# Eight heads instead of four per group in a decode attention kernel: 8 MiB V tiles, K in two halves, a mask for the own head

## The chip, the cores and the metric

The kernel runs on one core of a Trainium2 chip. The core has a matrix engine (TensorE, PE in the profile, with its weight loads as PEld), a vector engine (VectorE, DVE), a scalar engine (ScalarE, ACT), a general engine (GpSimd, POOL), and a queue engine (SyncE, SP) that here only issues transfers. Sixteen DMA engines move data from the device memory (HBM) into the on-chip memory of 128 partitions (SBUF). PE writes to the accumulator memory PSUM. The metric is the device time of one execution in microseconds, lower is better.

## The reference, cut to what matters

One decode step for 8 sequences: attention over a cache of 4096 keys and 32 heads of width 128, gated against a small MLP on the same x.

```
B, Sq, D = 8, 1, 576
H, Sk, Dh = 32, 4096, 128
q = (x @ wq).reshape(B, Sq, H, Dh).transpose(0, 2, 1, 3)
scores = einsum("bhqd,bhkd->bhqk", q, k_cache) * (Dh ** -0.5)
o = einsum("bhqk,bhkd->bhqd", softmax(scores), v_cache)
a = o.transpose(0, 2, 1, 3).reshape(B, Sq, H * Dh) @ wo
b = gelu(layernorm(x) @ w1 + b1) @ w2 + b2
out = g * a + (1 - g) * b          # g = sigmoid(sum(x * gate_w))
```

K and V caches are bf16, 268.4 MB each. All weights together are some 20 MB. With one query per sequence every byte of K and V is used once.

## The kernel before, in words

A group g is one batch row and HB = 4 heads; NG = 64 groups, batch row innermost. K and V of a group are 4 MiB each. They lie in SBUF with a head on 32 partitions, 128 consecutive keys on each partition (NTT = 128), so that one partition row is 32 KB and contiguous in HBM, and the whole tile is one contiguous stretch of 4 MiB. There are two buffers for K (KB) and two for V (VB).

The instructions of each engine stand in an order written out by hand; `op` records them, with the producers that each waits for. For a group:

- `q_of`: PE spreads q of the group's four heads over the partitions with a selection matrix, ACT copies it to q_bc.
- `scores`: the keys are worked in four chunks of 32 keys per partition. Per chunk, `mult` lets DVE multiply K by q (L354, 128x4096 elements) into one of the two halves of p1, PE sums that in eight matmuls against the identity (L364), and `reduce` lets DVE add the last 16 values (L369) into s_sb. The fourth multiply of a group frees its K buffer (`k_done`).
- `softmax`: DVE takes the maximum of each head (L387 to L393), then ACT runs four exp, one per head and its 32 partitions (L396), into P. P holds for each key a row of four head columns, of which only the own head's is ever written; the others stay zero from a memset at the start.
- `rowsum`, `total`: DVE sums P over the keys (L402), PE adds over partitions (L421).
- `pv`: PE multiplies P with V in 32 matmuls of 16 columns by 512 (L414); the last one frees the V buffer (`v_done`). `evict` copies the result out (L427), `gather` picks the own head's rows in four matmuls (L432), `norm` divides (L438, L439).

These steps are staggered: `rowsum`, `total`, `pv` and `evict` of group g-1 run inside the scores of group g, `norm` of g-2 too.

The transfers of K and V (`load_k` L223, `load_v` L229) stand in SP's one queue. At group g, K of g+1 is issued (it waits until K of g-1 is used up), then V of g (it waits for `pv` of g-2). SP issues strictly in order.

The MLP and the two projections ride along: `up_proj` in groups 3 to 14, `act_h` and the load of w2 at group 15, `down_proj` in groups 19 to 24, `b_out` and the load of wo at group 25, `a_proj` for each set of four heads once all batch rows are normalised. The weights share the buffer RB one after another.

At the end, V of the last group comes in seven pieces of falling size (V_LAST: 32, 32, 16, 16, 16, 8, 8 keys per partition). It is used by `pv_turned` (L508), which makes V the stationary operand and P the four moving columns, one matmul per key row, 128 in all, so that its result needs no gather. After the last piece come `norm_turned` (L517), the last `a_proj` (L477), the final mix (L593) and four small stores.

Of the kernel before, what the change touches and what calls it, by code (L numbers as in the profile page):

```python
# [11 lines left out]
B = 8  # L12
# [9 lines left out]
HB = 4  # L22
NHG = H // HB
NG = NHG * B
NTT = SK // 32
CT = 32
NCK = NTT // CT
# [5 lines left out]
NTQ = NTT // TQ  # L33

# [50 lines left out]
def bass_gated_mix__mha_block_cached__mixer_channel_mlp__decode_kernel(  # L85
# [41 lines left out]
    p1 = sb("p1", [128, 2, CT, DH], BF16)  # L127

# [20 lines left out]
    up = sb("up", [128, 2, NJ * B], F32)  # L149
    Q4 = sb("Q4", [128, NHG * DH], BF16)  # L150
    Sel = sb("Sel", [128, B, 128], BF16)
    q_bc = sb("q_bc", [128, 2, DH], BF16)
    OT_sb = sb("OT_sb", [128, H, B], BF16)
    bmg_sb = view(up, 0, [128, QN])
# [4 lines left out]
    sel16 = sb("sel16", [128, TQ, HB], F32)  # L159
    stat = sb("stat", [B, 16], F32)  # L160
    s_sb = sb("s_sb", [128, 2, NTT], F32)
# [3 lines left out]
    mD = sb("mD", [128, 2, 32], F32)  # L165
    gm = sb("gm", [128, 1], F32)
    P = sb("P", [128, 2, NTT, HB], BF16)
    rs = sb("rs", [128, 2, HB], F32)
# [14 lines left out]
    sV = [nc.alloc_semaphore(f"sV{i}") for i in range(2)]  # L183
    nK, nV = [0, 0], [0, 0]
# [8 lines left out]
    def bcast(t):  # L193
# [6 lines left out]
    ld_b2 = [load("scalar", b2_4[32 * i:32 * i + B, :],  # L200
                  bass.AP(tensor=B_b2.tensor, offset=B_b2.offset + i * QN, ap=[[0, B], [1, QN]]), f"ld_b2{i}", [c_b2])
             for i in range(4)]
# [9 lines left out]
    def kv_src(cache, g):  # L212
        hg, b = divmod(g, B)
        return cache[b, hg * HB:(hg + 1) * HB].rearrange("h (p t) d -> (h p) t d", p=32)

# [3 lines left out]
    def load_k(g):  # L219
        s = g % 2  # L220
        nK[s] += 1
        src = kv_src(A_k_cache, g)
        k_land[g] = op("sync", lambda e: e.dma_start(KB[s][:, :, :], src), [k_done.get(g - 2)], dma=(sK[s], 16 * nK[s]))  # L223

    def load_v(g):
        s = g % 2
        nV[s] += 1
        src = kv_src(A_v_cache, g)
        t = op("sync", lambda e: e.dma_start(VB[s][:, :, :], src), [v_done.get(g - 2)], dma=(sV[s], 16 * nV[s]))  # L229
        v_land[g] = [(t, 0, NTT)]  # L230
# [3 lines left out]
    def load_v_pieces(g):  # L234
        s = g % 2
        src = kv_src(A_v_cache, g)
        v_land[g] = []
        t0 = 0
        for n, nt in enumerate(V_LAST):
            dst, part = VB[s][:, t0:t0 + nt, :], src[:, t0:t0 + nt, :]  # L240
            t = load("sync", dst, part, f"sVl{n}", [v_done.get(g - 2)])
            v_land[g].append((t, t0, t0 + nt))
            t0 += nt
        assert t0 == NTT

    load_k(0)
    load_v(0)
    load_k(1)


    def memset(engine, ap, value):
# [9 lines left out]
    c_P = memset("gpsimd", P[:], 0.0)  # L261
    c_ps = [memset("vector", bank[i][:, :], 0.0) for i in range(4)]
    c_yps = memset("vector", y_ps[:, :], 0.0)
    c_sel16 = op("vector", lambda e: e.tensor_reduce(
        out=sel16[:].rearrange("p t h -> p (t h)"),
        in_=bass.AP(tensor=ident, offset=0, ap=[[pstride(ident), 128], [1, TQ * HB], [32, 4]]),
        axis=AX.X, op=ALU.add), [c_id])
    c_Sel = op("vector", lambda e: e.tensor_copy(
        out=Sel[:].rearrange("p b (h r) -> p b h r", h=HB),
        in_=bass.AP(tensor=ident, offset=0, ap=[[pstride(ident), 128], [1, B], [32, HB], [0, 32]])), [c_id])  # L270
# [54 lines left out]
    for half in range(2):  # L325
        for h in range(HB):
            for kt in range(NKT):
                o = tr_ps[half][32 * h:32 * h + B, :]
                at = (kt * SK + half * (SK // 2) if kt < NKF else NKF * SK) + h * DH
                r = bass.AP(tensor=RB, offset=at, ap=[[pstride(RB), 128], [HB * DH, 4], [1, DH]])  # L330
# [11 lines left out]
    a_qb, v_mult, v_red, p_sum, v_nm, a_exp, p_pv, a_ev, p_oz, v_norm, v_rs, p_z, v_rz = ({} for _ in range(13))  # L342

    def q_of(g):
        hg, b = divmod(g, B)
        t = op("tensor", lambda e: e.matmul(qb_ps[:, 0:DH], lhsT=Sel[:, b, :], rhs=Q4[:, hg * DH:(hg + 1) * DH],  # L346
                                            start=True, stop=True), [a_Q[hg // 4], c_Sel, a_qb.get(g - 1)])
        a_qb[g] = op("scalar", lambda e: e.activation(out=q_bc[:, g % 2, :], in_=qb_ps[:, 0:DH], func=ACT.Copy),  # L348
                     [t, v_mult.get((g - 2, NCK - 1))])

    def mult(g, c):
        s, par = g % 2, c % 2
        qb = bass.AP(tensor=q_bc, offset=q_bc[:, s, :].offset, ap=[[pstride(q_bc), 128], [0, CT], [1, DH]])
        v_mult[g, c] = op("vector", lambda e: e.tensor_tensor(  # L354
            out=p1[:, par, :, :], in0=KB[s][:, c * CT:(c + 1) * CT, :], in1=qb, op=ALU.mult),
            [k_land[g], a_qb[g], p_sum.get((g, c - 2) if c >= 2 else (g - 1, c + NCK - 2))]
            + ([v_yT, p_yT, p_Q] if g == 0 and c < 2 else []))
        if c == NCK - 1:
            k_done[g] = v_mult[g, c]
        for n in range(NCH):  # L360
            r = bass.AP(tensor=p1, offset=p1[:, par, 0, n * CH:n * CH + 1].offset,
                        ap=[[pstride(p1), 128], [DH, CT], [1, CH]])
            w = [v_mult[g, c], v_red.get((g, c - 2) if c >= 2 else (g - 1, c + NCK - 2)), *a_Q] if n == 0 else ()
            p_sum[g, c] = op("tensor", lambda e, r=r, n=n: e.matmul(  # L364
                tr_ps[par][:, :], lhsT=ident[:, :], rhs=r, start=(n == 0), stop=(n == NCH - 1)), w)

    def reduce(g, c):
        s, par = g % 2, c % 2
        v_red[g, c] = op("vector", lambda e: e.tensor_reduce(  # L369
            out=s_sb[:, s, c * CT:(c + 1) * CT], in_=tr_ps[par][:, :].rearrange("p (t c) -> p t c", c=CH),  # L370
            axis=AX.X, op=ALU.add), [p_sum[g, c], a_exp.get(g - 2)])

    def scores(g, between):

        mult(g, 0)
        between(0)
        mult(g, 1)
        between(1)
        for c in range(NCK):
            reduce(g, c)  # L380
            if c + 2 < NCK:
                mult(g, c + 2)
                between(c + 2)

    def softmax(g):
        s = g % 2
        t = op("vector", lambda e: e.tensor_reduce(out=mA[:, 0:1], in_=s_sb[:, s, :], axis=AX.X, op=ALU.max),  # L387
               [v_red[g, NCK - 1], c_mA])
        t = op("vector", lambda e: e.transpose(mB[:, :], mA[:, :]), [t])  # L389
        t = op("vector", lambda e: e.tensor_reduce(out=gm[:, :], in_=mB[:, :], axis=AX.X, op=ALU.max), [t])  # L390
        gmb = bass.AP(tensor=gm, offset=0, ap=[[pstride(gm), 128], [0, 32]])
        t = op("vector", lambda e: e.tensor_scalar(out=mC[:, :], in0=gmb, scalar1=-1.0, scalar2=None, op0=ALU.mult), [t])
        v_nm[g] = op("vector", lambda e: e.transpose(mD[:, s, :], mC[:, :]), [t, a_exp.get(g - 2)])  # L393
        for h in range(HB):
            q = slice(32 * h, 32 * h + 32)
            a_exp[g] = op("scalar", lambda e, h=h, q=q: e.activation(  # L396
                out=P[q, s, :, h], in_=s_sb[q, s, :], func=ACT.Exp, bias=mD[q, s, 0:1], scale=1.0),
                [v_nm[g], p_pv.get(g - 2), v_rs.get(g - 2), c_P])

    def rowsum(g):  # L400
        s = g % 2
        v_rs[g] = op("vector", lambda e: e.tensor_reduce(  # L402
            out=rs[:, s, :], in_=P[:, s, :, :].rearrange("p t h -> p h t"), axis=AX.X, op=ALU.add),
            [a_exp[g], p_z.get(g - 2)])

    def pv(g, part, parts):
        s = g % 2
        for land, t0, t1 in v_land[g]:
            t0, t1 = max(t0, part * NTT // parts), min(t1, (part + 1) * NTT // parts)
            for tq in range(t0 // TQ, t1 // TQ):  # L410
                j = tq % 4
                o = o_ps[s][32 * j:32 * j + TQ * HB, :]
                w = [land, a_exp[g], a_ev.get(g - 2), *c_ps] if tq == t0 // TQ else ()
                p_pv[g] = op("tensor", lambda e, o=o, tq=tq: e.matmul(  # L414
                    o, lhsT=P[:, s, tq * TQ:(tq + 1) * TQ, :].rearrange("p t h -> p (t h)"),
                    rhs=VB[s][:, tq * TQ:(tq + 1) * TQ, :].rearrange("p t d -> p (t d)"),
# [216 lines left out]
```

## Time and profile before

| | |
|---|---|
| runs of the kernel, median (lowest to highest) | 1310.96 us (1310.36 to 1311.30) |
| span of the profiled execution, first to last instruction | 1308.8 us |
| HBM bytes read | 556.96 MB |
| mean rate over the span | 426 GB/s |
| DVE / PE / ACT busy | 66% / 64% / 16% |
| mean granted PE clock | 0.818 |

The profiled execution's own time is its span; the median of the runs is 2.16 us above that span. The page of the profile gives the busy time of each engine, the span in 40 slices, the DMA queues, the chain of work that ended last, the costliest groups of instructions and the DMA issues. In a row of a group, the first figure after the bar is the busy time in us, the second the mean of one instruction in ns, and what follows the second bar is the engine's idle time just before them and what ended it.

### The profile page before, as it was taken

What the parts mean: (1) busy time and instruction counts of PE and PEld (TensorE: products, weight loads), DVE (VectorE), ACT (ScalarE), POOL (GpSimd) and SP (SyncE); (2) the same over time, 40 slices, a digit from 0 to 9 for tenths busy, and PEclk for the clock granted to TensorE, in tenths of its full rate; (3) what the DMA queues carried; (4) which work ended last, traced back from release to release, by engine and by line L of the source; (5) the groups of instructions that cost most, each with busy time, mean ns of one, the idle gap of its engine ahead of it and who ended that gap; (6) DMA issues with size and microseconds to landing.
All of it is one profiled execution on the core that took longest, in us unless ns stands there. A gap on an engine that the chain in (4) does not pass through costs nothing.

```text
span 1308.8 us, 12641 instructions
## 1 busy us (share of the span) xinstructions
PE 843.5 (64%) x5428; PEld 384.4 (29%) x5428; DVE 869.7 (66%) x1061; ACT 204.1 (16%) x393; POOL 2.5 (0%) x13
## 2 busy tenths in 40 slices
PE   3567766766746666646766766765766665766766
PEld 1223433433312233212322222322322222322323
DVE  4576676676747667646766766766776666776675
ACT  1201111111210110101011111011111111111111
POOL 0000000000000000000000000000000000000000
PEclk8878888878868888768878878878878878878878
DMA  9999999999999999999999999999999999999997
GB/s 398 422 431 432 431 432 431 432 431 430 434 424 432 430 431 429 428 418 432 429 431 429 431 431 431 431 432 430 432 430 431 431 431 429 432 431 432 429 420 311
DMA packets 25255, 557.77 MB, mean 426 GB/s; under 512 B 2528, under 2 KB 6640, under 8 KB 7536
## 3 DMA queue, kind: packets, MB, share of 16 engines
q1 hardware_dynamic: 24944, 556.95, 99.4%
q8 instruction: 42, 0.69, 0.2%
q14 instruction: 13, 0.11, 0.0%
q10 hardware_dynamic: 256, 0.03, 0.0%
HBM read 556.96 MB, written 0.01 MB: 426 GB/s over the span
## 4 chain that ended last, share of the span: by engine, by line
DMA 69%; DVE 20%; PE 10%; SPq 0%; issue 0%; ACT 0%
DMA KB<-in_A_k_cache_dram 68%; DVE p L354 16%; PE psb L364 10%; DVE s_sb L369 3%; DMA VB<-in_A_v_cache_dram 1%; SPq L187 0%; PE psb L414 0%; ACT L467 0%; SPq L229 0%; DVE mA L387 0%; SPq L223 0%; PE psb L477 0%; DVE mB L389 0%; ACT O_sb L427 0%; DVE gm L390 0%
## 5 line engine op out<-in xcount | busy, mean ns | idle before, releaser
L364 PE MATMUL psb<-p,ident 128*128 128x512 bf16 x2048 | 610.9, 459 | 412.2 <-DVE p L354 411.8
L354 DVE TENSOR_TENSOR p<-KB,q_bc 128x4096 bf16<-128x4096 bf16 x256 | 579.6, 2285 | 278.0 <-DMA KB<-in_A_k_cache_dram 278.0
L364 PEld LDWEIGHTS psb<-p,ident 128*128 128x128 bf16 x2048 | 218.1, 114 | 744.5 <-DVE p L354 445.2
L369 DVE TENSOR_REDUCE s_sb<-psb 128x32 f32<-128x512 f32 x256 | 176.1, 688 | 129.9 <-PE psb L364 129.6
L427 ACT ACTIVATE O_sb<-psb 128x512 f32<-128x512 f32 x63 | 37.6, 597 | 1032.2 <-PE psb L414 1032.2
L396 ACT ACTIVATE P<-s_sb,mD 32x128 bf16<-32x128 f32 x256 | 147.0, 574 | 12.9 <-DVE mD L393 9.0
L414 PE MATMUL psb<-VB,P 128*16 128x512 bf16 x2016 | 119.9, 379 | 0.3 <-DMA VB<-in_A_v_cache_dram 0.3
L432 PE MATMUL psb<-sel,O_sb 128*128 128x4 f32 x504 | 66.9, 256 | 32.9 <-ACT O_sb L427 32.9
L432 PEld LDWEIGHTS psb<-sel,O_sb 128*128 128x128 f32 x504 | 61.6, 192 | 41.3 <-ACT O_sb L427 41.2
L414 PEld LDWEIGHTS psb<-VB,P 128*16 128x16 bf16 x2016 | 44.7, 89 | 70.4 <-issue 26.3
L402 DVE TENSOR_REDUCE rs<-P 128x4 f32<-128x512 bf16 x64 | 43.5, 680 | 2.1 <-ACT P L396 2.1
L421 PEld LDWEIGHTS psb<-rs,ones 128*128 128x128 f32 x128 | 24.4, 192 | 9.3 <-issue 0.4
L348 ACT ACTIVATE q_bc<-psb 128x128 bf16<-128x128 f32 x64 | 17.4, 272 | 32.7 <-PE psb L346 32.7
L452 PEld LDWEIGHTS psb<-yT_sb,RB 128*128 128x128 bf16 (+1 forms) x216 | 19.4, 165 | 3.4
L452 PE MATMUL psb<-yT_sb,RB 128*128 128x8 bf16 (+1 forms) x216 | 19.8, 227 | 0.0
L387 DVE TENSOR_REDUCE mA<-s_sb 128x1 f32<-128x128 f32 x64 | 18.3, 286 | 2.2
L421 PE MATMUL psb<-rs,ones 128*128 128x4 f32 x128 | 18.4, 214 | 0.0
L389 DVE STREAM_TRANSPOSE mB<-mA 128x32 f32<-128x32 f32 x64 | 13.6, 213 | 2.2
L393 DVE STREAM_TRANSPOSE mD<-mC 128x32 f32<-128x32 f32 x64 | 13.6, 212 | 2.2
L346 PE MATMUL psb<-Q,Sel 128*128 128x128 bf16 x64 | 14.7, 229 | 0.0
L346 PEld LDWEIGHTS psb<-Q,Sel 128*128 128x128 bf16 x64 | 6.1, 96 | 27.0 <-issue 26.8
L390 DVE TENSOR_REDUCE gm<-mB 128x1 f32<-128x32 f32 x64 | 11.9, 186 | 2.2
(63 smaller groups left out, 84.7 us busy)
## 6 DMA issues: line engine op xcount, KB each, us to landing
KB<-in_A_k_cache_dram SPq DMA_DIRECT2D x64, 4096.0 KB, 27.2
VB<-in_A_v_cache_dram SPq DMA_DIRECT2D x63, 4096.0 KB, 33.1
RB<-in_B_w_dram SPq DMA_DIRECT2D x1, 5184.0 KB, 44.3
RB<-in_B_w_dram SPq DMA_DIRECT2D x1, 4608.0 KB, 36.6
RB<-in_A_wo_dram SPq DMA_DIRECT2D x1, 4608.0 KB, 44.7
RB<-in_A_wq_dram SPq DMA_DIRECT2D x1, 4096.0 KB, 12.8
VB<-in_A_v_cache_dram SPq DMA_DIRECT2D x2, 1024.0 KB, 8.7
VB<-in_A_v_cache_dram SPq DMA_DIRECT2D x3, 512.0 KB, 11.2
```

What stands on the lines that cost most here:

```text
L346: t = op("tensor", lambda e: e.matmul(qb_ps[:, 0:DH], lhsT=Sel[:, b, :], rhs=Q4[:, hg * DH:(hg + 1) * DH], start=True, stop=True), [a_Q[hg ...
L354: v_mult[g, c] = op("vector", lambda e: e.tensor_tensor(out=p1[:, par, :, :], in0=KB[s][:, c * CT:(c + 1) * CT, :], in1=qb, op=ALU.mult), ...
L364: p_sum[g, c] = op("tensor", lambda e, r=r, n=n: e.matmul(tr_ps[par][:, :], lhsT=ident[:, :], rhs=r, start=(n == 0), stop=(n == NCH - 1)), w)
L369: v_red[g, c] = op("vector", lambda e: e.tensor_reduce(out=s_sb[:, s, c * CT:(c + 1) * CT], in_=tr_ps[par][:, :].rearrange("p (t c) -> p t ...
L387: t = op("vector", lambda e: e.tensor_reduce(out=mA[:, 0:1], in_=s_sb[:, s, :], axis=AX.X, op=ALU.max), [v_red[g, NCK - 1], c_mA])
L396: a_exp[g] = op("scalar", lambda e, h=h, q=q: e.activation(out=P[q, s, :, h], in_=s_sb[q, s, :], func=ACT.Exp, bias=mD[q, s, 0:1], scale=1.0),
L402: v_rs[g] = op("vector", lambda e: e.tensor_reduce(out=rs[:, s, :], in_=P[:, s, :, :].rearrange("p t h -> p h t"), axis=AX.X, op=ALU.add), ...
L414: p_pv[g] = op("tensor", lambda e, o=o, tq=tq: e.matmul(o, lhsT=P[:, s, tq * TQ:(tq + 1) * TQ, :].rearrange("p t h -> p (t h)"), rhs=VB[s] ...
L421: p_z[g] = op("tensor", lambda e: e.matmul(oz_ps[:, HB:2 * HB], lhsT=ones[:, :], rhs=rs[:, g % 2, :], start=True, stop=True), [v_rs[g], v_ ...
L427: a_ev[g] = op("scalar", lambda e: e.activation(out=O_sb[:].rearrange("p t d -> p (t d)"), in_=o_ps[s][:, :], func=ACT.Copy), [p_pv[g], p_ ...
L432: p_oz[g] = op("tensor", lambda e, tt=tt: e.matmul(oz_ps[:, 0:HB], lhsT=O_sb[:, tt, :], rhs=sel16[:, tt, :], start=(tt == 0), stop=(tt == ...
L452: st["p_up"] = op("tensor", lambda e, w=w, o=o, kt=kt: e.matmul(o, lhsT=w, rhs=yT_sb[:, kt, :], start=(kt == 0), stop=(kt >= NKF)), [*ld_w ...
```

## The change

HB becomes 8, so there are 32 groups n. A head now has 16 partitions, with 256 consecutive keys on each (NTT = 256).

- V of a group is one transfer of 8 MiB with 64 KB per partition, into one buffer of that size; there is no second V buffer. V of n+1 waits until `pv` of n is done.
- K of a group comes in two halves of the keys (units u = 2n and 2n+1), each 4 MiB with 32 KB rows that lie 64 KB apart in HBM. The two K buffers stay as they were; the first half's buffer is free after the fourth multiply, the second's after the eighth.
- `scores` runs eight chunks. `softmax` has one exp over all 128 partitions and 256 keys into E; then DVE multiplies E eight times by a column of `own` (1 where the partition belongs to the head, else 0), which writes all eight head columns of P. The row sum is one reduce of E and a multiply with `own`.
- `pv` has 64 matmuls with 32 columns; `total`, `pv`, `evict` and `gather` of a group now follow its softmax at once, before the next group's scores; `norm` comes in the next group's second chunk.
- q is broadcast once per batch row for all 32 heads (8 times instead of 64).
- SP's order at the end of group n: both halves of K of n+1, then V of n+1. At the start K0, K1, V0. In the last two groups: first half of V of 30, both K halves of 31, second half of V of 30, first half of V of 31 into the first K buffer, then the seven pieces with the second half of V of 31 into VB.
- At the end: `pv_turned` has 256 matmuls with eight moving columns; the last `a_proj` covers eight heads.
- To make room, P of the last group lies in p1, the MLP's scratch in Q4, and the loads of b2 come later (group 9). The MLP keeps its places, counted in units u.

The core of the diff:

```diff
-HB = 4
+HB = 8
+RH = 128 // HB
...
-NTT = SK // 32
+NTT = SK // RH
+NKH = 2
+NTK = NTT // NKH
...
-    KB = [sb(f"KB{i}", [128, NTT, DH], BF16) for i in range(2)]
-    VB = [sb(f"VB{i}", [128, NTT, DH], BF16) for i in range(2)]
+    KB = [sb(f"KB{i}", [128, NTK, DH], BF16) for i in range(NKH)]
+    VB = sb("VB", [128, NTT, DH], BF16)
...
+    def load_k(u):
+        n, s = divmod(u, NKH)
+        src = kv_src(A_k_cache, n)[:, s * NTK:(s + 1) * NTK, :]
...
+    def load_v(n):
+        t = op("sync", lambda e: e.dma_start(VB[:, :, :], src), [v_done.get(n - 1)], dma=(sV, 16 * nV[0]))
...
+        a_exp[n] = op("scalar", lambda e: e.activation(
+            out=E[:, :], in_=s_sb[:, :], func=ACT.Exp, bias=mD[:, 0:1], scale=1.0), [v_nm[n], ...])
         for h in range(HB):
-            a_exp[g] = op("scalar", lambda e, h=h, q=q: e.activation(
-                out=P[q, s, :, h], in_=s_sb[q, s, :], func=ACT.Exp, bias=mD[q, s, 0:1], scale=1.0), [...])
+            v_P[n] = op("vector", lambda e, h=h: e.tensor_scalar(
+                out=(P if n < NG - 1 else P_last)[:, :, h, :], in0=E[:, :].rearrange("p (q t) -> p q t", t=TQ),
+                scalar1=own[:, h:h + 1], scalar2=None, op0=ALU.mult), [...])
...
+        scores(n, between)
+        softmax(n)
+        if n < last:
+            total(n)
+        if n < last - 1:
+            load_k(NKH * (n + 1))
+            load_k(NKH * (n + 1) + 1)
+            pv(n, (0,))
+            evict(n)
+            gather(n)
+            if n + 1 < last - 1:
+                load_v(n + 1)
+        if n == last - 2:
+            load_v_part(last - 1, VB, 0, 0, NTK, [v_done[n]])
+        if n == last - 1:
+            load_k(NKH * last)
+            load_k(NKH * last + 1)
+            load_v_part(n, VB, NTK, NTK, NTT, [v_done[n - 1]])
+            pv(n, (0,))
...
+    pv(last - 1, (1,))
     evict(last - 1)
     pv_turned(last, (0,))
     gather(last - 1)
     norm(last - 1)
     total(last)
     recip(last)
-    pv_turned(last, range(2, len(V_LAST)))
+    pv_turned(last, range(1, 1 + len(V_LAST)))
     norm_turned(last)
```

More of the change, by code (lines that the diff above doesn't have):

```diff
@@ L325, in bass_gated_mix__mha_block_cached__mixer_channel_mlp__decode_kernel @@
     for half in range(2):
-        for h in range(HB):
+        for h in range(4):
             for kt in range(NKT):
@@ L367, in reduce, with q_of @@
[L367 to L375, printed above, removed]
+    a_qb, v_mult, v_red, p_sum, v_nm, a_exp, v_P, p_pv, a_ev, p_oz, v_norm, v_rs, p_z, v_rz = ({} for _ in range(14))
+    def q_of(b):
+        for i in range(2):
+            t = op("tensor", lambda e, i=i: e.matmul(
+                qb_ps[64 * i:64 * i + 64, :], lhsT=Sel[:, b, :],
+                rhs=bass.AP(tensor=Q4, offset=i * DH, ap=[[pstride(Q4), 128], [2 * DH, NHG], [1, DH]]),
+                start=True, stop=True), [*a_Q, c_Sel, a_qb.get(b - 1)] if i == 0 else ())
+        a_qb[b] = op("scalar", lambda e: e.activation(out=q_bc[:, b, :], in_=qb_ps[:, :], func=ACT.Copy), [t])
@@ L480, in quarters, with load_b2 @@
         return last
+    def load_b2():
+        st["ld_b2"] = [
+            load("scalar", b2_4[32 * i:32 * i + B, :],
+                 bass.AP(tensor=B_b2.tensor, offset=B_b2.offset + i * QN, ap=[[0, B], [1, QN]]), f"ld_b2{i}", [c_b2])
+            for i in range(4)]
     def down_proj(j0, j1):
```

338 lines of the change are left out of this document (157 added, 181 removed).

## The prediction

> **What bounds the kernel now.** I read the page first (busy shares, slices, queues, chain), then the groups, then the timeline of one group, last the end of the span.
>
> ```profile
> span 1308.8 us, 12641 instructions
> GB/s 398 422 431 432 431 432 431 432 431 430 434 424 432 430 431 429 428 418 432 429 431 429 431 431 431 431 432 430 432 430 431 431 431 429 432 431 432 429 420 311
> q1 hardware_dynamic: 24944, 556.95, 99.4%
> DMA 69%; DVE 20%; PE 10%; SPq 0%; issue 0%; ACT 0%
> ...
> L354 DVE TENSOR_TENSOR p<-KB,q_bc 128x4096 bf16<-128x4096 bf16 x256 | 579.6, 2285 | 278.0 <-DMA KB<-in_A_k_cache_dram 278.0
> L369 DVE TENSOR_REDUCE s_sb<-psb 128x32 f32<-128x512 f32 x256 | 176.1, 688 | 129.9 <-PE psb L364 129.6
> L427 ACT ACTIVATE O_sb<-psb 128x512 f32<-128x512 f32 x63 | 37.6, 597 | 1032.2 <-PE psb L414 1032.2
> L396 ACT ACTIVATE P<-s_sb,mD 32x128 bf16<-32x128 f32 x256 | 147.0, 574 | 12.9 <-DVE mD L393 9.0
> ...
> KB<-in_A_k_cache_dram SPq DMA_DIRECT2D x64, 4096.0 KB, 27.2
> ...
> RB<-in_B_w_dram SPq DMA_DIRECT2D x1, 5184.0 KB, 44.3
> ...
> RB<-in_A_wo_dram SPq DMA_DIRECT2D x1, 4608.0 KB, 44.7
> ```
>
> The transfers bound it. Their queue is busy 99.4% of the span, the rate stands at 431 GB/s from slice 20 to 37, and DVE idles 278 us for K. A K tile lands 27.2 us after its issue, while 4 MiB at 431 GB/s take 9.73 us: nearly two tiles are always waiting ahead of it. No engine's work matters unless it lets that queue run dry or lies behind the last byte.
>
> **Compute, removed and added.** One four-chunk tile on DVE and its queues:
>
> ```profile
> 600.41 4.49 DVE L354 TENSOR_TENSOR p<-KB,q_bc 128x4096 bf16<-128x4096 bf16 x2 [3.70 <-DMA KB<-in_A_k_cache_dram]
> ...
> 607.00 2.28 DVE L354 TENSOR_TENSOR p<-KB,q_bc 128x4096 bf16<-128x4096 bf16 x1
> ...
> 609.80 2.28 DVE L354 TENSOR_TENSOR p<-KB,q_bc 128x4096 bf16<-128x4096 bf16 x1
> ...
> 612.11 0.33 SPq L223 DMA_DIRECT2D KB<-in_A_k_cache_dram  x1
> ...
> 613.97 1.90 PE L414 MATMUL psb<-VB,P 128*16 128x512 bf16 x32
> 614.08 0.69 DVE L369 TENSOR_REDUCE s_sb<-psb 128x32 f32<-128x512 f32 x1 [1.39 <-PE psb L364]
> ...
> 615.81 0.21 DVE L393 STREAM_TRANSPOSE mD<-mC 128x32 f32<-128x32 f32 x1
> ```
>
> The third multiply starts 6.6 us after the first, each further one 2.80 us later, and the last reduce ends 4.97 us after the fourth multiply starts (614.77). Eight chunks in a row take 6.6 + 5 x 2.80 + 4.97 = 25.6 us. The maximum chain takes 1.25 us (614.77 to 616.02), with 256 keys some 0.15 more. The one exp of 256 elements lies between the 574 ns above (128 elements) and the 597 ns of a 128x512 eviction: 0.6. The mask is new. Its nearest rows, from the list of groups and that of one line:
>
> ```profile
> L392 DVE TENSOR_SCALAR mC<-gm 128x32 f32<-128x32 f32 x64 | 11.6, 182 | 2.2
> ```
> ```profile
> L464 DVE TENSOR_SCALAR up<-up x1: 309/309/309, 334.6 to 334.6; 128x288 f32<-128x288 f32 x1
> ```
>
> Eight of about 0.31 make 2.5 us (at 182 ns, the price of a tiny one, 1.5). So P is ready 25.6 + 1.4 + 0.6 + 2.5 = 30.1 us after the first K half lands; DVE is free at 30.7. The 192 dropped exp, 56 dropped q broadcasts and 31 dropped evictions sit on ACT, 16% busy: worth nothing here.
>
> **Does the queue run dry?** Per group 16 MiB pass in 38.9 us. Count from the landing of K's first half: second half 9.7, V 29.2, next K halves 38.9 and 48.7. P is ready at 30.1, 64 PV matmuls take 2 x 1.90, so V of n+1 is issued at about 34, with 14.7 us of K still queued. Behind that waiting V on SP stands K of n+2, whose buffer comes free only at 38.9 + 11.7 = 50.6: nothing is held up. PE's scores of n+1 stand behind PV of n, and end that wait at about 35.5 (eviction and gather), before K at 38.9. The DMA engines do not run level, though:
>
> ```profile
> 1286.00:1288.00 2.00, 2.00 (x16) 0.77 (x18) 2.00 (x2) 0.00 (x0) 0.00 (x0) 1.00 0.84 360
> 1288.00:1290.00 2.00, 2.00 (x31) 0.81 (x24) 2.00 (x3) 0.47 (x1) 0.00 (x0) 1.00 0.53 221
> ...
> 1294.73 1.90 PE L414 MATMUL psb<-VB,P 128*16 128x512 bf16 x32 [0.33 <-DMA VB<-in_A_v_cache_dram]
> ```
>
> The last column of these stretches is the rate, the one before it the share of the 16 DMA engines. Near the end some engines are out of work from 1287 on (shares 0.84 and 0.53) although the same tile lands complete at 1294.7: a lead of about 7.5 us, so the real cover is 14.7 - 7.5 = 7 us. Without it, every microsecond of lateness would cost some 30. I take 0.
>
> **Fewer packets.** The 24944 packets are 22680 rows plus 16 for each of 143 transfers (24 fewer, as three tiny ones have 8 rows): a row is one packet, even w2's of 41 KB (5184 KB over 128). V's rows fall from 8960 to 5120, 240 fewer per DMA engine, and 30 transfers fall away. The price comes from the load of wo, 4096 rows of 1152 B:
>
> ```profile
> 555.00:560.00 5.00, 3.86 (x20) 1.78 (x18) 4.61 (x4) 0.00 (x0) 0.00 (x0) 0.99 0.99 375
> 560.00:565.00 5.00, 4.10 (x43) 1.51 (x41) 3.43 (x8) 0.08 (x1) 0.00 (x0) 1.00 1.08 391
> 565.00:570.00 5.00, 1.08 (x9) 0.97 (x8) 0.02 (x1) 2.98 (x6) 0.00 (x0) 0.87 1.15 418
> ```
>
> It loses (56 + 40 + 13) x 5 / 431 = 1.26 us for 256 packets per engine where 32 KB rows would need 9: 5.1 ns each. So 240 fewer save 1.2 us. Ends: 0, if 64 KB rows travel as two packets, and 2.6, if besides each of the 30 transfers saves 45 ns (the seven last pieces take 1304.7 - 1294.7 = 10.0 us against 9.73, over six extra ends). [...]
>
> **The end.** There the last byte no longer covers PE:
>
> ```profile
> 1293.44 0.95 PE L432 MATMUL psb<-sel,O_sb 128*128 128x4 f32 x8
> ...
> 1295.62 2.34 ACT L396 ACTIVATE P<-s_sb,mD 32x128 bf16<-32x128 f32 x4 [5.49 <-DVE mD L393]
> ...
> 1298.11 0.94 PE L508 MATMUL psb<-P,VB 128*128 128x4 bf16 x32 [1.16 <-ACT P L396]
> ...
> 1298.91 1.62 PE L432 MATMUL psb<-sel,O_sb 128*128 128x4 f32 x8
> ...
> 1300.57 0.18 DVE L438 RECIPROCAL rz<-psb 128x4 f32<-128x4 f32 x1 [1.89 <-PE psb L432]
> ...
> 1301.25 0.57 PE L421 MATMUL psb<-rs,ones 128*128 128x4 f32 x2
> ...
> 1301.67 1.17 PE L508 MATMUL psb<-P,VB 128*128 128x4 bf16 x32
> ...
> 1303.47 1.00 PE L508 MATMUL psb<-P,VB 128*128 128x4 bf16 x24 [0.63 <-DMA VB<-in_A_v_cache_dram]
> ...
> 1304.72 0.38 PE L508 MATMUL psb<-P,VB 128*128 128x4 bf16 x8 [0.25 <-DMA VB<-in_A_v_cache_dram]
> ...
> 1305.37 0.65 PE L477 MATMUL psb<-RB,OT_sb 128*8 128x144 bf16 x16 [0.27 <-DVE OT_sb L517]
> ```
>
> Call the last landing T (1304.7 now). P is ready at T - 6.8 and PE keeps up, ending the turned matmuls at T + 0.4. After the change, K of the last group lands at T - 10.0 - 3 x 9.73 = T - 39.2. The group before got its K 29.2 us earlier and needs 30.7 of DVE, so DVE starts 1.5 us late and P is ready at T - 39.2 + 1.5 + 30.1 = T - 7.6. From there PE has, one after another: 128 turned matmuls at about 33 ns (32 in 0.94 to 1.17 us) 4.2, gather 1.6, the wait for norm on DVE 0.5, total 0.6, and 128 more, 4.2: 11.1 us, to T + 3.5 instead of T + 0.4. The last projection has 16 more matmuls: 0.4. Together +3.5 us. Ends: 29 ns and a gather of 0.95 give +1.8, 42 ns (24 in 1.00) and 0.65 for the projection give +6.1; a P one us earlier or later shifts both.
>
> **Sum.** 3.5 - 1.2 = +2.3 us on a span of 1308.8: 1311.1. The median stands 2.16 above that execution's span, so 1313.3. The first K half still lands first; w1 comes behind 4 MiB more but ahead of group 1's K, so before unit 3 needs it; w2 and wo keep their place behind V: nothing. The four loads of b2 move from the start of ACT's queue to group 9:
>
> ```profile
> 1.36 1.37 ACTq L187 DMA_DIRECT2D b<-in_B_b_dram  x4
> ```
>
> 1.4 us of ACT's queue, covered by ACT's idle time (84% of the span); in the way of an exp it would use a fifth of the 7 us cover.
>
> **Rivals.**
>
> ```profile
> 0.00:2.00 2.00, 0.00 (x0) 0.00 (x0) 0.97 (x3) 0.00 (x0) 1.24 (x10) 1.00 0.03 9
> ```
>
> (1) No net change, 1311: PE's last stretch mostly hides. It decides if P is ready at about T - 10 (PE then ends at T + 1.1: 0.7 + 0.4 - 1.2 = 0); a mask at 182 ns gives 1.0 of the 2.4 us. For it: mask and exp are unmeasured. Against: 25.6 us of the 30.1 come from measured rows. (2) Faster, the other side, 1307.2: the ends of transfers are where bytes are lost. Then 2.6 us go, and up to 1.8 more (0.6% idle of the queue is 7.9 us; 2 of them pass before the first bytes, by the row above, and 4.1 behind the last landing); with only 0.6 left of the tail that is -3.8. It decides once the saving exceeds the tail's 3.5. Against it: one transfer's end is already overlapped by the next two in the queue. (3) Slower, 1320: the new steps between addresses (64 KB per partition instead of 32) slow HBM itself. Half a percent of 431 GB/s, about what sustained slices differ by (429 to 432), costs 6.5 us. No row here has that step. [...] (4) The single V buffer starves the queue: if P is over 7 us later than worked out, each further one costs 30 us, 1340 or so.
>
> **Chances.** The forecast (end grows, 1312 to 1317) 0.50, of which 0.35 beyond +0.2%; rival 1 0.15; rival 2 0.23; rival 3 0.08; rival 4 0.04. Faster 0.23, same 0.30, slower 0.47, where 0.2% (2.6 us) is about what a measurement of this kernel can tell from no change. The range 1305.5 to 1320 leaves out the far part of rivals 2 to 4; the forecast's own is 1311 to 1317.
>
> **What would show it.** Queue packets of about 20,600 if 64 KB rows stay whole (24,500 if split); slices still at 431; V issues some 34 us after the first K half's landing; the second lot of 128 turned matmuls running past the last landing by about 3.5 us without waiting for DMA; the last projection near 1.1 us. Wrong it would be if slices leave 431, or if the last turned matmuls wait for V as now.

## The result: 2.2 us faster, where 2.3 us slower was forecast

Over 19 runs each, on the same chips, the kernel before took 1310.63 us (median, 1310.14 to 1311.42) and the changed kernel 1308.43 us (1308.23 to 1309.09). The ratio is 0.9983, with a 95% interval of 0.9977 to 0.9990. The change is real, and about the size of the 0.2% that was named as the limit of such a measurement. The prediction, 1313.3 us, had the wrong sign; its range, 1305.5 to 1320, holds the time.

The lines of the page after that answer to those shown of before:

```profile
span 1306.6 us, 11660 instructions
...
GB/s 399 417 452 422 440 422 433 432 439 428 436 420 443 430 421 431 432 420 430 436 425 432 431 447 418 433 429 433 437 434 436 423 430 433 432 432 444 417 405 321
...
q1 hardware_dynamic: 20624, 556.95, 99.3%
q8 instruction: 40, 0.66, 0.2%
...
q14 instruction: 11, 0.09, 0.0%
...
DMA 69%; DVE 20%; PE 9%; issue 0%; SPq 0%; ACT 0%
...
L361 DVE TENSOR_TENSOR p<-KB,q_bc 128x4096 bf16<-128x4096 bf16 x256 | 582.3, 2285 | 328.7 <-DMA KB<-in_A_k_cache_dram 328.7
...
L406 DVE TENSOR_SCALAR P<-E,own 128x256 bf16<-128x256 bf16 x248 | 51.5, 283 | 17.8 <-ACT E L403 17.8
...
L403 ACT ACTIVATE E<-s_sb,mD 128x256 bf16<-128x256 f32 x32 | 16.2, 508 | 776.7 <-DVE mD L402 776.7
```

The queue of the transfers (q1) is still busy for 99.3% of the span, with 20624 packets, as forecast for 64 KB rows that stay whole: 4320 fewer, or 270 for each DMA engine. The slices no longer stand flat at 431 GB/s: between the third and the 38th they swing from 417 to 452 around it. Where V again travels in 32 KB rows (below), they are flat again. The prediction named slices that leave 431 as a sign against it. But a slice (32.7 us) counts a packet whole where it starts, and sixteen packets of 64 KB are 32 GB/s of a slice, so the counting alone can make such swings; the queue's share of the span did not fall by more than 0.1 points. The page calls q8 and q14 queues of instructions. The packets of q8 are 16 KB, and 2816 more instructions of PE brought 11 more of them (pe_more, below); those of q14 are 8 KB, and 720 more of DVE brought 5 (extra_after, below). Of q14's 11, nine are DVE's and two are put down to ACT and SP, by the instructions after which they come. Before, each of the two queues had two packets more:

```profile
q8 instruction: 42, 0.69, 0.2%
q14 instruction: 13, 0.11, 0.0%
```

The end of the changed kernel, in its timeline (start, duration, engine and line; in brackets the idle time before and what ended it):

```profile
1289.99 1.66 DVE L406 TENSOR_SCALAR p<-E,own 128x256 bf16<-128x256 bf16 x8 [0.57 <-ACT E L403]
...
1292.06 3.45 PE L520 MATMUL psb<-p,KB 128*128 128x8 bf16 x128 [2.92 <-DMA KB<-in_A_v_cache_dram]
...
1295.37 1.85 PE L439 MATMUL psb<-selO,O_sb 128*128 128x8 f32 x8
...
1298.20 3.58 PE L520 MATMUL psb<-p,VB 128*128 128x8 bf16 x120
...
1302.03 0.38 PE L520 MATMUL psb<-p,VB 128*128 128x8 bf16 x8 [0.25 <-DMA VB<-in_A_v_cache_dram]
...
1302.69 1.13 PE L484 MATMUL psb<-RB,OT_sb 128*8 128x144 bf16 x32 [0.29 <-DVE OT_sb L529]
```

The last eight turned matmuls wait for the last piece of V, as they did before. So PE is not late, and the end still hangs on the last landing T. T moved from 1304.7 to 1302.0 us, by -2.7; what follows T grew from 4.1 to 4.6 us, by the last projection (1.13 instead of 0.65 us). -2.7 + 0.5 = -2.2. Nothing is gained at the end itself: the last landing of the same K bytes (the second K half of a group) is ahead of before by 0.2 us near the start of the run, 0.55 after a quarter of the groups, 1.4 after half, 2.2 after three quarters, and 2.6 in the last group (groups beside which a load of weights has moved are left out).

### The profile page after: what moved, and what is told of

The parts are those of the page before. It is cut to its first block, busy times and chain, and to the rows that moved or that the text cites. A ratio compares the mean times of both kernels' runs of the same rounds, so it can differ in the third digit from the quotient of the medians.

```text
span 1306.6 us, 11660 instructions
## 1 busy us (share of the span) xinstructions
PE 809.4 (62%) x5156; PEld 342.7 (26%) x5156; DVE 856.2 (66%) x1094; ACT 47.9 (4%) x81; POOL 1.6 (0%) x12
## 3 DMA queue, kind: packets, MB, share of 16 engines
q1 hardware_dynamic: 20624, 556.95, 99.3%
## 4 chain that ended last, share of the span: by engine, by line
DMA 69%; DVE 20%; PE 9%; issue 0%; SPq 0%; ACT 0%
DMA KB<-in_A_k_cache_dram 68%; DVE p L361 17%; PE psb L371 9%; DVE s_sb L377 3%; DMA VB<-in_A_v_cache_dram 2%; SPq L198 0%; PE psb L421 0%; DVE P L406 0%; PE psb L484 0%; PE psb L428 0%; ACT E L403 0%; DVE mA L394 0%; PE psb L520 0%; DVE out_sb L606 0%; DVE es L409 0%
## 5 line engine op out<-in xcount | busy, mean ns | idle before, releaser
L371 PE MATMUL psb<-p,ident 128*128 128x512 bf16 x2048 | 544.3, 417 | 297.1 <-DVE p L361 296.9
L371 PEld LDWEIGHTS psb<-p,ident 128*128 128x128 bf16 x2048 | 197.6, 105 | 622.2 <-DVE p L361 384.9
L421 PE MATMUL psb<-VB,P 128*32 128x512 bf16 x1984 | 175.9, 532 | 0.7 <-DMA VB<-in_A_v_cache_dram 0.7
L428 PE MATMUL psb<-rs,ones 128*128 128x8 f32 x64 | 18.8, 367 | 156.6 <-DVE rs L410 156.1
L421 PEld LDWEIGHTS psb<-VB,P 128*32 128x32 bf16 x1984 | 64.3, 129 | 97.4 <-issue 80.9
L406 DVE TENSOR_SCALAR P<-E,own 128x256 bf16<-128x256 bf16 x248 | 51.5, 283 | 17.8 <-ACT E L403 17.8
L439 PE MATMUL psb<-selO,O_sb 128*128 128x8 f32 x248 | 33.6, 262 | 21.2 <-ACT O_sb L434 21.2
L403 ACT ACTIVATE E<-s_sb,mD 128x256 bf16<-128x256 f32 x32 | 16.2, 508 | 776.7 <-DVE mD L402 776.7
L439 PEld LDWEIGHTS psb<-selO,O_sb 128*128 128x128 f32 x248 | 30.8, 195 | 36.0 <-ACT O_sb L434 36.0
L434 ACT ACTIVATE O_sb<-psb 128x512 f32<-128x512 f32 x31 | 18.5, 596 | 258.7 <-PE psb L421 258.7
```

Of the source, the lines that this page charges most:

```text
L371: fn = lambda e, r=r, i=i: e.matmul(tr_ps[par][:, :], lhsT=ident[:, :], rhs=r, start=(i == 0), stop=(i == NCH - 1))
L403: a_exp[n] = op("scalar", lambda e: e.activation(out=E[:, :], in_=s_sb[:, :], func=ACT.Exp, bias=mD[:, 0:1], scale=1.0), [v_nm[n], v_P.get ...
L406: v_P[n] = op("vector", lambda e, h=h: e.tensor_scalar(out=(P if n < NG - 1 else P_last)[:, :, h, :], in0=E[:, :].rearrange("p (q t) -> p ...
L421: p_pv[n] = op("tensor", lambda e, o=o, tq=tq, at=at, buf=buf: e.matmul(o, lhsT=P[:, tq, :, :].rearrange("p h t -> p (h t)"), rhs=buf[:, a ...
L428: p_z[n] = op("tensor", lambda e: e.matmul(oz_ps[:, HB:2 * HB], lhsT=ones[:, :], rhs=rs[:, :], start=True, stop=True), [v_rs[n], v_norm.ge ...
L434: a_ev[n] = op("scalar", lambda e: e.activation(out=O_sb[:].rearrange("p t d -> p (t d)"), in_=o_ps[s][:, :], func=ACT.Copy), [p_pv[n], p_ ...
```

## The experiments

"After" is the changed kernel, 1308.43 us, and every figure with a sign is against it. The kernel before took 1310.5 to 1310.6 us beside each of them, and a ratio is the run's time over that. Of each edit the core is shown; "..." marks what is left out.

**V in 32 KB rows again (v_rows32).** Two transfers by keys for each V tile, in groups 0 to 29; all else as after.

```diff
-        t = op("sync", lambda e: e.dma_start(VB[:, :, :], src), [v_done.get(n - 1)], dma=(sV, 16 * nV[0]))
...
+        for i in range(2):
+            t0, t1 = i * NTT // 2, (i + 1) * NTT // 2
+            t = op("sync", lambda e, t0=t0, t1=t1: e.dma_start(VB[:, t0:t1, :], src[:, t0:t1, :]),
+                   [v_done.get(n - 1)], dma=(sV[i], 16 * nV[0]))
...
```

> The changed kernel, but V of groups 0 to 29 comes as two transfers of 4 MiB (keys 0 to 127 and 128 to 255 of each partition): 32 KB rows again, and 30 transfers more; all else is kept. Packet theory (every row is a packet that costs its DMA engine some 11 ns beside its bytes): 240 packets more per engine make 2.6 us, 30 ends at 9 ns 0.3, so 1311.3 against 1308.4, the whole gain gone. Prediction's price (5.1 ns): 1309.9. Ends theory (the gain came from 30 fewer transfer ends, 90 ns each): 1311.1.

```profile
GB/s 401 416 434 432 432 432 431 432 431 430 430 433 433 425 431 431 431 418 428 431 430 431 426 431 432 429 431 432 432 432 431 432 431 430 430 432 431 430 403 323
...
q1 hardware_dynamic: 24944, 556.95, 99.4%
```

1310.69 us (1310.36 to 1311.14), ratio to before 1.0001 [0.9992, 1.0009], +2.3 us: the whole gain is gone, with 24944 packets again, and T is 1304.15. This leaves open whether the packets or the 30 more transfers cost it.

**V in one transfer, but in rows of 32 KB (v_gap512).** A gap of 512 bytes in SBUF between the two halves of a partition's row forces two packets for each, with no transfer more.

```diff
-    VB = sb("VB", [128, NTT, DH], BF16)
+    VGAP = 256
+    VB = sb("VB", [128, NTT * DH + VGAP], BF16)
...
+        dst = bass.AP(tensor=VB, offset=0, ap=[[pstride(VB), 128], [NTK * DH + VGAP, 2], [1, NTK * DH]])
+        src2 = src.rearrange("p (a t) d -> p a (t d)", a=2)
...
```

> As the run with the two halves of a V row 32 bytes apart, but 512 bytes apart, so that the tensors allocated behind V in SBUF stay on their alignment: in that run the 1152-byte rows of wo, whose tensor it had moved by 32 bytes, took 54 to 62 ns each instead of 51, which is 1.3 us over 256 of them per engine. Packets: 3840 more than in the changed kernel, no transfer more. Packet theory: 2.2 us, 1310.6. If the gap itself costs, 1311.9 again. Ends theory: 1308.4.

```profile
q1 hardware_dynamic: 24464, 556.95, 99.3%
...
VB<-in_A_v_cache_dram SPq DMA_DIRECT2D x30, 8192.0 KB, 32.4
```

1310.69 us (1310.38 to 1311.18), ratio 1.0001 [0.9992, 1.0010], +2.26 us. Still 30 transfers of 8 MiB (second row), but 240 packets more for each DMA engine, and the gain is gone. So the ends of transfers are not what was saved; the packets are, at 2.26 / 240 = 9.4 ns each. A first version of this edit (v_gap) had a gap of 32 bytes instead:

> The changed kernel, but the two halves of a V row lie 32 bytes apart in SBUF, so that the one 8 MiB transfer of V in groups 0 to 29 has two pieces of 32 KB per partition instead of one of 64 KB: 3840 packets more (about 24464 in all), not one transfer more. Packet theory, at the 9.2 ns a packet that the runs with 32 KB and 16 KB rows gave (6.6 us for 720 packets): 2.2 us, 1310.6. Ends theory (the gain lies in the number of transfers): 1308.4.

It took 1311.95 us, +3.5. That gap also shifted the tensor of wo by 32 bytes in SBUF, and its packets of 1152 bytes took 54 to 62 ns instead of 51, so this run can't be read for the packets alone.

**V in 16 KB rows, and K in 16 KB rows (v_rows16, k_rows16).** Four transfers of 64 keys for each V tile; or, in another kernel, two for each K half (the edit shown).

```diff
-        k_land[u] = op("sync", lambda e: e.dma_start(KB[s][:, :, :], src), [k_done.get(u - NKH)], dma=(sK[s], 16 * nK[s]))
+        k_land[u] = [op("sync", lambda e, j=j: e.dma_start(KB[s][:, 64 * j:64 * j + 64, :], src[:, 64 * j:64 * j + 64, :]),
+                        [k_done.get(u - NKH)], dma=(sK[s][j], 16 * nK[s])) for j in range(2)]
...
```

> The changed kernel, but V of groups 0 to 29 comes as four transfers of 64 keys: 16 KB rows, 11520 packets more (720 per engine) and 90 transfers more. Packet theory: 7.9 + 0.8 = 8.7 us, 1317.1. Prediction's price (5.1 ns): 3.7 + 0.5, 1312.6.

> The changed kernel with every K half in two transfers of 64 keys: 16 KB rows, 8192 packets more (512 per engine) and 64 transfers more; V as in the changed kernel. Packet theory at 9.2 ns: 4.7 us, 1313.1. If V's long rows were special, for instance because V lies in one stretch in HBM: nearer to 1308.4.

The first row is the queue with V in 16 KB rows:

```profile
q1 hardware_dynamic: 33584, 556.95, 99.5%
```

and this one with K in them:

```profile
q1 hardware_dynamic: 29840, 556.95, 99.4%
```

V: 1315.47 us (1315.24 to 1315.62), ratio 1.0037 [1.0024, 1.0050], +7.0 us for 810 packets more per engine, 8.7 ns each. K: 1313.35 us (1312.97 to 1314.12), ratio 1.0022 [1.0013, 1.0031], +4.9 us for 576, 8.5 ns each. With v_rows32 (2.26 us for 270 packets, 8.4 ns each) the price holds from 64 KB down to 16 KB rows and for either tensor.

**Fewer packets still (w_rows).** The four row blocks of wq and of w1 are laid out so that each partition reads four neighbouring rows, as one packet instead of four (only the expressions that change are shown).

```diff
-A_wq[0:512, :].rearrange("(kt p) n -> p kt n", p=128)
+A_wq[0:512, :].rearrange("(p kt) n -> p kt n", p=128)
-B_w1[0:512, :].rearrange("(kt p) f -> p kt f", p=128)
+B_w1[0:512, :].rearrange("(p kt) f -> p kt f", p=128)
-i = src[:, kt * 128:(kt + 1) * 128] if kt
+i = src[:, 0:512].rearrange("b (p k) -> b k p", k=NKF)[:, kt, :] if kt
```

> The changed kernel with wq and w1 laid out so that a partition takes four neighbouring rows of the weight in one piece (32 and 36 KB instead of 8 and 9 KB; x and its normalised form are split over the partitions the same way): 768 packets fewer, 48 per engine. Packet theory: 0.4 us less, 1308.0. Ends theory: 1308.4.

```profile
q1 hardware_dynamic: 19856, 556.95, 99.3%
```

1307.99 us (1307.68 to 1308.31), ratio 0.9980 [0.9971, 0.9989], -0.44 us for 48 packets fewer per engine: 9.2 ns each. This is the fastest kernel that does the whole computation, ahead of before and, by less than the intervals can tell apart, of after.

**V in two transfers of 64 partitions (v_parts).** More transfers, the rows whole.

```diff
+        t = [op("sync", lambda e, i=i: e.dma_start(VB[64 * i:64 * i + 64, :, :], src[64 * i:64 * i + 64]),
+                [v_done.get(n - 1)], dma=(sV[i], 16 * nV[0])) for i in range(2)]
...
```

> The changed kernel, but V of groups 0 to 29 comes as two transfers of 64 partitions each: the rows stay 64 KB and as many as in the changed kernel, and there are 30 transfers more. Packet theory: 30 more completion writes per engine at 9 ns, 0.3 us, 1308.7. Ends theory (90 ns an end): 1311.1, as slow as before. This run tells the two apart.

```profile
GB/s 325 348 248 245 274 277 284 277 277 252 233 329 272 277 249 229 268 312 273 243 244 274 268 246 267 192 231 253 267 175 262 239 266 177 244 235 266 193 289 337
```

2232.94 us (2143.5 to 2241.0); the shortest, which is the one profiled, is 64% over before. None of the theories had that: a miss for what it was meant to tell. A packet of 64 KB took 5.05 us in the mean instead of 2.42, and the mean rate over the span was 260 GB/s. Why a packet takes twice as long when a transfer covers 64 partitions was not shown; no other run here tries it.

**The masks of the last group twice (mask_last2).** P of the last group becomes ready later.

```diff
-        for h in range(HB):
+        for r, h in [(r, h) for r in range(2 if n == NG - 1 else 1) for h in range(HB)]:
...
```

> The changed kernel with the eight mask multiplies of the last group done twice, so that its P is ready 1.7 us later. If PE's last stretch was hidden by only 0.25 us, the end moves by 1.0 to 1.4 us: 1309.4 to 1309.8. If the tail has cover to spare: 1308.4.

```profile
1289.28 3.35 DVE L406 TENSOR_SCALAR p<-E,own 128x256 bf16<-128x256 bf16 x16 [0.58 <-ACT E L403]
...
1292.78 3.56 PE L520 MATMUL psb<-p,KB 128*128 128x8 bf16 x128 [4.35 <-DVE p L406]
...
1299.02 3.55 PE L520 MATMUL psb<-p,VB 128*128 128x8 bf16 x128
```

1308.86 us (1308.58 to 1310.33), ratio 0.9989 [0.9980, 0.9997], +0.4 us. All 128 turned matmuls of the second half now run in one row with no wait for V: PE ends at 1302.57, 0.6 behind T (1301.97). In this profile P is ready 1 us later than in that of after, and PE ends 0.2 us later; the median of the runs rose by 0.4, less than the 1.0 to 1.4 expected, and not clear of the intervals. So it is the trace that shows it: the chain that the prediction feared exists, and in the changed kernel it ends just before it would count.

**Later P in the other groups (mask_x4, mask_x2, extra_after, late_big).** The masks four times, or twice, in groups 0 to 29 (the same edit with another condition).

> The changed kernel with the mask multiplies of groups 0 to 29 done four times, so that P of each is ready some 5 us later; the last two groups are as they were. If the single V buffer leaves a cover of about 7 us, as the prediction had it, the time stays: 1308.4. If the cover is below 5 us, each microsecond that lacks costs about 30: 1320 or more.

> The changed kernel with the mask multiplies of groups 0 to 29 done twice: P of each 1.7 us later instead of 5. Cover theory (the lead that the faster DMA engines have gathered, up to 7.5 us, is eaten only when the queue behind a V issue gets shorter than that; with 5 us it was 8.6 us long, with 1.7 it is 10.4): 1308.4 to 1309. Proportional theory (every microsecond of P costs 0.035 us a group, the changed kernel has a loss of this kind too): 1310.1.

Four times: 1313.76 us (1312.98 to 1314.44), ratio 1.0023 [1.0014, 1.0032], +5.3. Twice: 1310.22 us (1309.87 to 1311.02), ratio 0.9998 [0.9990, 1.0007], +1.8. P is 5.1 and 1.7 us later, so this looked like a price of about one microsecond, over the whole run, for each microsecond of lateness in a group. My theory, a cover of 7 us, said nothing or little; the other, a queue that runs dry, some 30 us for each. Neither fits. But these kernels also have 720 and 240 more vector instructions, and 5 and 2 more reads on q14. Two kernels part these causes. One (extra_after) makes the same 24 extra instructions per group behind the row sum, where P does not wait for them:

```diff
+        for h in range(24 if n < NG - 2 else 0):
+            v_ex[n] = op("vector", lambda e, h=h: e.tensor_scalar(
+                out=P_last[:, :, h % HB, :], in0=E[:, :].rearrange("p (q t) -> p q t", t=TQ),
+                scalar1=own[:, h % HB:h % HB + 1], scalar2=None, op0=ALU.mult), [v_ex.get(n, v_rs[n])] if h % HB == 0 else ())
```

> 24 more vector instructions of the mask's form per group in groups 0 to 29, as many as with the masks four times, but behind the row sum instead of ahead of P: P is not later, only the engine's idle time ahead of the next K is filled. If the 5.3 us of the masks four times come from the instructions themselves (their fetches, their traffic), about 1313.4 (+5) again. If they come from P's lateness, no change: 1308.4, within 0.5.

```profile
q14 instruction: 16, 0.13, 0.0%
```

1313.51 us (1313.09 to 1314.03), ratio 1.0023 [1.0014, 1.0033], +5.1, with 16 reads on q14, as with the masks four times. The other (late_big) makes P late by two large multiplies ahead of the softmax:

```diff
     def softmax(n):
+        for i in range(2 if n < NG - 2 else 0):
+            v_ex[n] = op("vector", lambda e: e.tensor_tensor(
+                out=p1[:, 0, :, :], in0=p1[:, 0, :, :], in1=bass.AP(tensor=q_bc, offset=0, ap=[[pstride(q_bc), 128], [0, CT], [1, DH]]),
+                op=ALU.mult), [v_ex.get(n, v_red[n, NC - 1])])
...
```

> Two large multiplies of 2.29 us in scratch ahead of the softmax in groups 0 to 29: P, and so the issue of the next V, is 4.6 us later, with only 60 more instructions instead of 720. If lateness costs by itself, as the masks four times suggest (5.3 us for 5.1 us of delay), about 1313.2 (+4.8). If the instructions cost, +0.4: 1308.8. My own theory of 7 us of cover says no change.

1308.26 us (1307.93 to 1308.83), ratio 0.9983 [0.9975, 0.9992], -0.2. One group in the timeline of the changed kernel:

```profile
609.02 4.49 DVE L361 TENSOR_TENSOR p<-KB,q_bc 128x4096 bf16<-128x4096 bf16 x2 [21.31 <-DMA KB<-in_A_k_cache_dram]
...
644.26 0.33 SPq L236 DMA_DIRECT2D VB<-in_A_v_cache_dram  x1
...
647.95 4.49 DVE L361 TENSOR_TENSOR p<-KB,q_bc 128x4096 bf16<-128x4096 bf16 x2 [9.26 <-DMA KB<-in_A_k_cache_dram]
```

and of the one with the two multiplies:

```profile
608.95 4.50 DVE L363 TENSOR_TENSOR p<-KB,q_bc 128x4096 bf16<-128x4096 bf16 x2 [17.00 <-DMA KB<-in_A_k_cache_dram]
...
647.85 4.50 DVE L363 TENSOR_TENSOR p<-KB,q_bc 128x4096 bf16<-128x4096 bf16 x2 [4.61 <-DMA KB<-in_A_k_cache_dram]
...
648.80 0.33 SPq L236 DMA_DIRECT2D VB<-in_A_v_cache_dram  x1
```

V is issued 4.5 us later, 0.95 us after the next group's first K half has landed, and the run loses nothing. So 4.5 us of lateness are free here, and the 5 us come from the 24 instructions in each group, wherever they stand. It is not what they write: the two large multiplies write more (8192 elements per partition in a group instead of 6144), and with them q14 stays at 11 reads.

**More matrix-engine instructions (pe_more).** Eight small matmuls more in each chunk of groups 8 to 29, 2816 instructions with their weight loads, in PE's idle time.

```diff
+            if B <= n < NG - 2:
+                for i in range(8):
+                    op("tensor", lambda e: e.matmul(qb_ps[:, 0:HB], lhsT=ident[:, :], rhs=ident[:, 0:HB],
+                                                    start=True, stop=True), [a_qb[B - 1]])
```

> The changed kernel with 1408 small extra matmuls (eight per chunk in groups 8 to 29, into a PSUM bank that is free by then), in PE's idle time; they add 2816 instructions, about 11 fetches of 16 KB beside the 40 there are. If fetches slow single DMA engines and the slowest one sets the end (its lag of 7.5 us at the end over 40 fetches): 2 us, 1310.5. If they spread evenly over 16 engines at 1.07 us each: 0.7, 1309.1. If fetches cost nothing: 1308.4.

```profile
q8 instruction: 51, 0.84, 0.3%
```

1310.57 us (1310.28 to 1311.00), ratio 1.0000 [0.9991, 1.0009], +2.1 us: instructions that nothing waits for, but 11 more reads of 16 KB through q8.

**Fewer instructions (sum_one, sum_mask_one).** One of eight summing matmuls kept; then also one of eight masks.

```diff
+        nch = NCH if n >= NG - 2 else 1
-        for i in range(NCH):
+        for i in range(nch):
...
-        for h in range(HB):
+        for h in range(1 if 0 < n < NG - 2 else HB):
```

> One of the eight matmuls that sum a product of K and q is kept in groups 0 to 29; seven eighths of that sum are left out. That is 3360 matrix-engine instructions fewer (1680 matmuls, each with its weight load), some 13 fetches of 16 KB fewer. Theory: these fetches hold back eight or nine of the sixteen DMA engines by some 1.55 us each (1.07 of their own, 0.48 by which the data packet beside them is stretched), the vector engine's fetches hold back one. Then the engines that fetch for the matrix engine come 13 x 1.55 / 9 = 2.2 us closer to the fastest, the vector engine's one stays where it is, and the time falls by 0 to 2.2 us, by how far that one engine lags: 1306.2 to 1308.4. If the spread between the engines has nothing to do with fetches, the spread at the end stays 7.5 us with the same set of engines, and the time 1308.4.

> The same, and in groups 1 to 29 only the first of the eight masks is made (the other seven columns of P are left as group 0 had them): 203 vector instructions fewer besides, 1.6 fetches of 8 KB. At 1.06 us for each on the one engine that serves them, as the 24 extra instructions per group cost (5.3 us for 5 fetches), the time falls by another 1.1 to 1.7 us below the kernel with one matmul of eight if that engine is then the last; by nothing if it is not.

The instruction queues of the first:

```profile
q8 instruction: 27, 0.44, 0.1%
q14 instruction: 11, 0.09, 0.0%
```

and of the second:

```profile
q8 instruction: 27, 0.44, 0.1%
...
q14 instruction: 9, 0.07, 0.0%
```

The first took 1308.20 us (1308.03 to 1308.52), ratio 0.9982 [0.9974, 0.9991], -0.2; the second 1306.59 us (1306.28 to 1307.56), ratio 0.9971 [0.9960, 0.9982], -1.8. Thirteen reads fewer by PE bring next to nothing, two fewer by DVE then bring 1.6 us. The landings say why. For the second K half of group 30, this is when each of the sixteen DMA engines finished its share, in us against the last one of the changed kernel, sorted:

```
before        -5.2 -4.9 -4.8 -4.6 -4.5 -3.9 -3.5  0.3  1.9  2.0  2.0  2.1  2.2  2.2  2.2  2.6
after         -7.5 -7.5 -7.4 -7.1 -7.1 -7.1 -6.9 -1.8 -1.7 -1.7 -1.5 -0.3 -0.1  0.0  0.0  0.0
extra_after   -4.5 -4.4 -4.3 -4.3 -4.3 -4.1 -3.7 -2.1 -2.0 -1.9 -1.7 -0.6 -0.5 -0.5 -0.4  5.5
late_big      -5.2 -5.1 -5.1 -5.1 -5.0 -5.0 -4.8 -1.9 -1.9 -1.8 -1.8 -0.4 -0.2 -0.1 -0.1  0.8
pe_more       -7.5 -7.4 -7.3 -7.2 -7.2 -7.2 -6.8 -0.5 -0.2  1.1  1.2  1.2  1.3  1.3  1.3  1.4
sum_one       -7.9 -7.8 -7.8 -7.6 -7.6 -6.9 -6.7 -4.9 -3.4 -3.3 -3.3 -3.2 -3.2 -2.9 -2.8 -0.1
sum_mask_one  -8.0 -8.0 -7.9 -7.8 -7.7 -7.2 -7.0 -5.0 -3.5 -3.5 -3.4 -3.4 -3.3 -3.2 -3.0 -1.2
```

With more vector instructions (extra_after) a single engine falls 6 us behind the next one. With more matrix-engine instructions (pe_more) most of the nine engines on the right fall back together, while the seven on the left stay. With fewer of those (sum_one) eight of the nine come forward by 2.5 us in the mean and one stays; with fewer vector instructions too (sum_mask_one) that one comes forward. The packet records say which engines these are. A data packet beside a read of PE is stretched, in the changed kernel, by 503, 465, 465, 478, 547, 547, 482 and 489 ns, and then by nearly the same eight again. I read that as eight engines in turn; eight are also those that come forward in sum_one. In extra_after, of DVE's 14 reads the ten whose stretched packet can be followed to the end of its tile all lie on the engine that lands last. The lead of the seven engines is thus mostly the reading of instructions by the other nine, and the last of these ends the run.

## Why the prediction was wrong

**The packet's price was mis-sized, in "5.1 ns each. So 240 fewer save 1.2 us".** The edits above give 8.4 to 9.4 ns a packet over rows from 8 to 64 KB, so the 270 packets fewer are worth 2.3 to 2.5 us. The records of the packets show the same in small: 1216 ns (median) for 32 KB, 2421 for 64 KB, so two halves take 11 ns more than the whole, or 8 to 10 by the distance of their starts in a row (1213 to 1214 and 2418 ns). The 5.1 ns came from the load of wo, and for that load the landings nearly bear the figure out: it took 11.95 us from the last landing before it to its own, 1.0 more than its bytes at 4 MiB in 9.73 us, or 4 ns for each packet. The step that failed is that the price of packets of 1152 bytes was carried over to rows of 32 KB. Why a packet of a long row costs twice as much stays open.

**The tail was mis-sized, in "Together +3.5 us".** It cost 0.5, and these 3.0 us are most of the 4.5 between forecast and result. The path was the right one, as the doubled masks of the last group show, but its terms were too long. The eight masks took 1.66 us in a row instead of 2.5: one of them takes 283 ns by its own row, but in sequence they follow each other every 0.21 us. The group before took DVE 29.7 us instead of 30.7, and the last group's K landed at T - 39.85 instead of T - 39.2, so DVE started it 0.15 us late and not 1.5. P was therefore ready at T - 10.3 instead of T - 7.6, even ahead of the first half of V, for which PE then waited (1292.01, T - 10.0). From there the 128 turned matmuls took 3.45 us (27 ns each) where 4.2 were counted. Rival 1 named that point, "about T - 10", and PE's last stretch does hide from there on; with the true price of packets on top, the time fell. The range held the time only because its lower part, made for rival 2, reached below the time of before. The last projection is the one term that came as worked out, +0.5 where 0.4 was forecast.

**Not in the sum: fewer instructions to read.** With V back in 32 KB rows the time is that of before within 0.2 us, although the last projection is 0.5 us longer, so some 0.3 to 0.5 us come from elsewhere. The changed kernel makes two reads of instructions fewer on each of q8 and q14. By pe_more (2.1 us for 11) the two on q8 are worth 0.4. The two on q14 are ACT's, by the instructions after which they come (three reads before, one after; DVE has nine and SP one in both). Two of the three can be followed to an engine that lands 3.4 and 4.6 us ahead of the last, so they should be worth nothing. That no other part of the change has a share in this was not tried on its own. The counts of dropped work on ACT were slips without weight in the sum: 224 exp and 32 evictions fell away, not 192 and 31.

**The cover was right in effect and wrong in its arithmetic.** V was issued 35.2 us after the first K half's landing (34 forecast) and the queue never ran dry. But "the real cover is 14.7 - 7.5 = 7 us" took the lead of the seven engines off. In late_big V came 4.5 us later still, and the leading engines must have run out of work at times: their lead over the last landing of after shrank from 7.2 to 5.1 us, while the last engine, which sets the end, lost 0.8 us at that landing and nothing by the end (T 1301.99 and 1301.98). So these 2.1 us of lead were given up for nothing. What the whole cover is, and what each microsecond beyond it costs, was not tried, so the 30 us of rival 4 stay open.

**The rivals.** (2), the ends of transfers, had the sign and nearly the size (1307.2 for 1308.4), but not the cause: v_gap512 has no transfer more and is as slow as v_rows32. (3), slower HBM by the 64 KB steps of K, did not show: K has these steps in v_rows32 as well, and there T is not later than before. The forecast of packets, the whole 64 KB rows, and the last projection came true; "the second lot of 128 turned matmuls running past the last landing by about 3.5 us without waiting for DMA" did not, and "if the last turned matmuls wait for V as now" was the sign named for a wrong prediction.

## What to carry to other kernels

Where a queue of transfers is busy 99% of the time, count its packets and read the price of one from the records of packets of the sizes in question (here 8 to 11 ns, where the runs gave 8.4 to 9.4), not from packets of another size (4 to 5 ns at 1152 bytes). Price a short instruction in a row by its spacing in a row (0.21 us for the mask), not by its own duration (283 ns). Where the DMA engines run apart, ask what holds the last one back before taking their lead off a cover: here only the last one's lateness cost (in late_big the others lost 2.1 us of lead and the time moved by -0.2), and there the engines' instructions themselves were traffic (0.19 us for each read of PE, 1.0 for each of DVE).

## What the runs showed of the hardware that was not expected

In these runs the reading of instructions took time from the data. A read for PE is 16 KB, one for each 256 instructions (pe_more: 2816 more, 11 reads more), and takes 1.07 us (median) where a data packet of that size takes 0.61 (in k_rows16). One for DVE is 8 KB in 0.33 us. In the changed kernel the data packet that overlaps a read of PE is stretched by 0.46 to 0.55 us, and the one beside a read of DVE by 0.56 to 0.66 (eight of the nine reads). PE's reads, by the stretches that come round after eight, fall on eight DMA engines in turn, and 11 more cost 2.1 us, 0.19 each. DVE's fall on one engine, as its lone lag of 5.9 us behind the next in extra_after shows, and cost 5.1 us for 5, 1.0 each, or 0.8 by the two that sum_mask_one saves. Both prices come out, as an estimate from these figures, if a read holds up its engine by its own time and the stretch beside it: 11 / 8 x (1.07 + 0.50) = 2.2 us for PE, 5 x (0.33 + 0.66) = 5.0 us for DVE. A hundred small vector instructions cost this run about 0.7 us even in idle time (5.1 us for 720 in extra_after). In this kernel, whose queue of transfers is busy 99.3% of the span, a read on the engine that lands last is not hidden (1.0 us each in extra_after).
